# Products of zeros behind TensorE's groups in an attention and gated feed-forward kernel

## The chip, the cores and the metric

The kernel runs on one core of a Trainium2 chip. The metric is the device time of one execution in microseconds (us). TensorE is called PE, VectorE DVE, ScalarE ACT, GpSimd POOL and SyncE SP, as in the rows of the profile.

## The reference

Inputs are q, k and v of shape (4, 8, 768, 64) and three weight arrays. For each of 32 heads:

```python
k_sum = k.reshape(B, H, nb, 32, D).max(axis=3)      # 24 block summaries per head
v_sum = v.reshape(B, H, nb, 32, D).mean(axis=3)
scores_l = scale * q @ k.T, kept where |i - j| < 16, else -1e9
scores_s = scale * q @ k_sum.T + log(32)
a = softmax(concat(scores_l, scores_s))
attn = a @ concat(v, v_sum)
```

The heads are joined to x of shape (4, 768, 512), and then

```python
h = relu(x @ w_in)                                  # 512 -> 1024
conv[s] = w[0]*h[s-1] + w[1]*h[s] + w[2]*h[s+1]     # along the sequence
out = (h * sigmoid(conv)) @ w_out                   # 1024 -> 512
```

## The kernel before, in words

The work is cut into eight chunks `c` (four batches, two halves of 384 positions each). A chunk has four pairs of heads `p`, so there are 32 pairs `n`. One pair goes through these steps. `prep_pair` (L185) takes block maxima of k on DVE and puts windows and maxima into `kw`. `qk` (L231) makes 24 small products of 64 rows into the two banks `pq`. `softmax` (L252) works on DVE and ACT. `tr` (L285) makes three transposes on PE into `pt` for each half and copies them out as `aT`, on ACT or DVE. `av` (L299) makes 24 small products into `xp`, which ACT and DVE split into a high and a low half, `xh` and `xl`. `vmean_pair` (L204) makes block means of v, with one transpose `pv`.

A feed-forward unit `(c, u)` covers 128 of the 1024 hidden columns. `f1` (L370) makes twelve products (three for each of four blocks of x) into a bank with tag f1. `gate_conv` (L391) and `gate_mul` (L420) make the gate on ACT, DVE and POOL. `f2` (L438) accumulates 128 output rows over the eight hidden blocks in the bank with tag f2.

The weights come as 64-bit words. `decode` (L75) and `weights` (L110) turn each block into two 32-bit halves, with one ACT pass, three DVE passes, an ACT copy and a POOL subtraction. w_in is decoded from the prologue into chunk 0, w_out in chunks 0 and 1 (`OUT_AT`).

The program is written in the order: prologue (attention of chunk 0, pairs 0 to 3, L481 to L491), two early units of `f1` and the decoding of the first blocks (L493 to L504), then the loop over chunks (L538). In the loop the attention of chunk c+1 is written between the units of chunk c by `slot`, `slot_t` and `slot_av`. The framework's scheduler sets the order on each engine when it builds the program. It takes the earliest written instruction that its model holds ready, so groups of PE can interleave. On the chip each engine keeps that order, waits at semaphores and overtakes nothing. Loads are on SP's queue, the outputs and two constants on ACT's. There are eight banks of PSUM: two for `pq` (tag s), one for `pt`, one for `xp` (tag x), three for f1, one for f2.

At the very start DVE clears a tile `idle` of 128x512 bf16 and PE makes six products of it with itself into a bank of tag x (L68 to L72). Nothing reads them.

Of the kernel before, what the change touches and what calls it, by code (L numbers as in the profile page):

```python
# [7 lines left out]
F32 = mybir.dt.float32  # L8
# [8 lines left out]
P = 128  # L17
# [6 lines left out]
NK = WK + NB  # L24
SP = S + 2 * WIN
NP = H // 2
# [7 lines left out]
DEPTH = 2  # L34
# [6 lines left out]
EARLY_IN = 2  # L41

OUT_AT = (6, 7, 8, 9, 10, 10, 11, 12)
EARLY_AT = 3
NGROUP = NCHUNK * NP * 2

# [2 lines left out]
def attention_ffn(ctx, tc, qT, kT, vT, v4, w_in, cwT, w_out, mask8, ident_in, out):  # L49
    nc = tc.nc  # L50
    cp = ctx.enter_context(tc.tile_pool(name="cp", bufs=1))
    sp = ctx.enter_context(tc.tile_pool(name="sp", bufs=2))
    ps = ctx.enter_context(tc.tile_pool(name="ps", bufs=1, space=bass.MemoryType.PSUM))
# [3 lines left out]
    ident = cp.tile([P, P], F32, name="ident")  # L57
# [7 lines left out]
    raw_b = cp.tile([P, 6, 1024], U32, name="raw_b", tag="big_b")  # L65


    idle = sp.tile([P, 512], mybir.dt.bfloat16, tag="a", name="idle", bufs=DEPTH + 2)  # L68
    nc.vector.memset(idle, 0.0)
    pw = ps.tile([P, 512], F32, tag="x", name="pw")  # L70
    for i in range(6):
        nc.tensor.matmul(pw, idle[:, :P], idle, start=True, stop=True)  # L72


    def decode(out, words, n, name):  # L75
# [23 lines left out]
    def split_in(fc, t):  # L99
        weights(t, flat(win_hi, fc), flat(win_lo, fc), f"i{fc}")  # L100
# [6 lines left out]
    def split_out(fc, t):  # L107
        weights(t, wout_hi[:, fc, :], wout_lo[:, fc, :], f"o{fc}")
# [14 lines left out]
    for tag in ("xh", "xl"):  # L123
        t = sp.tile([P, 2, KL], F32, tag=tag, name=f"k_{tag}", bufs=2)
        spare += [t[:, 0, :], t[:, 1, :]]

    def window(ap, step, lead, run):

        return bass.AP(
            tensor=ap.tensor, offset=ap.offset, ap=[lead, [QB * step, CB], [1, run]]  # L130
        )
# [99 lines left out]
    def qk(c, p):  # L231


        st = state[(c, p)]
        n = c * NP + p
        pq = [
            ps.tile([P, 512], F32, tag="s", name=f"pq{n}_{h}", bufs=2) for h in range(2)
        ]
        for blk in range(CB):
            i, half = divmod(blk, 2)  # L240
            for h in range(2):
                r = slice(h * QB, (h + 1) * QB)
                nc.tensor.matmul(  # L243
                    pq[h][half * QB : (half + 1) * QB, i * NK : (i + 1) * NK],
                    st["q"][r, blk * QB : (blk + 1) * QB],
                    st["kw"][r, blk, :],
                    start=True,
                    stop=True,
                )
        softmax(n, c % 2, pq)  # L250

    def softmax(n, hf, pq):  # L252
        nm = sp.tile([P, 2, 3], F32, tag="nm", name=f"nm{n}", bufs=3)
        sm = sp.tile([P, 2, 3], F32, tag="sm", name=f"sm{n}", bufs=3)
        for h in range(2):
            a = sp.tile([P, 3, NK], F32, tag="a", name=f"a{n}_{h}", bufs=DEPTH + 2)
            state[("a", 2 * n + h)] = a
            for i in range(3):
                nc.vector.tensor_tensor_reduce(  # L259
                    a[:, i, :],  # L260
                    pq[h][:, i * NK : (i + 1) * NK],
                    mask[:, hf, i, :],
                    -0.125,
                    3.0e38,
                    ALU.add,
                    ALU.min,
                    nm[:, h, i : i + 1],
                )
                nc.scalar.activation(  # L269
                    a[:, i, :],  # L270
                    a[:, i, :],
                    AF.Exp,
                    bias=nm[:, h, i : i + 1],
                    scale=-1.0,
                    accum_out=sm[:, h, i : i + 1],
                )
        nc.scalar.activation(sm, sm, AF.Copy, bias=1e-9)
        nc.vector.reciprocal(sm, sm)
        for h in range(2):
            a = state[("a", 2 * n + h)]  # L280
            (nc.gpsimd if n >= NP else nc.vector).tensor_tensor(  # L281
                a, a, sm[:, h, :].unsqueeze(2).to_broadcast([P, 3, NK]), ALU.mult
            )

    def tr(j):  # L285
        a = state.pop(("a", j))
        pt = ps.tile([P, 512], F32, tag="t", name=f"pt{j}")
        for i in range(3):
            nc.tensor.transpose(pt[:NK, i * P : (i + 1) * P], a[:, i, :], ident)  # L289
        aT = sp.tile([P, 3 * P], F32, tag="aT", name=f"aT{j}", bufs=3)  # L290
        if j < 2 * NP and j % 2:
            nc.vector.tensor_copy(aT[:NK, :], pt[:NK, : 3 * P])
        else:
            nc.scalar.copy(aT[:NK, :], pt[:NK, : 3 * P])
        state[("aT", j)] = aT
# [3 lines left out]
    def av(n):  # L299
        c, p = divmod(n, NP)  # L300
        b, hf = divmod(c, 2)
        va = state[(c, p)]["va"]
        aT = [state.pop(("aT", 2 * n + h)) for h in range(2)]
        xp = ps.tile([P, 512], F32, tag="x", name=f"xp{n}")
        for blk in range(CB):
            for h in range(2):
                r = slice(h * QB, (h + 1) * QB)
                nc.tensor.matmul(  # L308
                    xp[r, blk * QB : (blk + 1) * QB],
                    va[:NK, blk, r],  # L310
                    aT[h][:NK, blk * QB : (blk + 1) * QB],
                    start=True,
                    stop=True,
                )
        if p == 0:
            xh = sp.tile([P, NCC, XW], F32R, tag="xh", name=f"xh{c}", bufs=2)
            xl = sp.tile([P, NCC, XW], F32R, tag="xl", name=f"xl{c}", bufs=2)
            xT[c] = (xh, xl)
            if hf:
                for n, o in zip(xT[c], xT[c - 1]):  # L320
                    nc.vector.tensor_copy(
                        n[:, :, 0:2], o[:, :, CH - 2 : CH].bitcast(F32)
                    )
        xh, xl = xT[c]
        o = 2 * hf
        nc.scalar.copy(xh[:, p, o : o + CH], xp[:, :CH])  # L326
        nc.vector.tensor_tensor(
            xl[:, p, o : o + CH],
            xp[:, :CH],
            xh[:, p, o : o + CH].bitcast(F32),  # L330
            ALU.subtract,
        )
# [25 lines left out]
    def slot_t(j):  # L358
        if 0 <= j - DEPTH < NGROUP:
            tr(j - DEPTH)  # L360
# [9 lines left out]
    def f1(c, fc, ccs):  # L370
        hf = c % 2
        n = CH + 2 * hf
        xh, xl = xT[c]
        if ccs[0] == 0:
            f1ps[(c, fc)] = ps.tile([P, 512], F32, tag="f1", name=f"f1_{c}_{fc}", bufs=3)
        ph = f1ps[(c, fc)]
        for cc in ccs:
            for m, (w, x) in enumerate(
                ((win_hi, xh), (win_hi, xl), (win_lo, xh))
            ):  # L380
                nc.tensor.matmul(  # L381
                    ph[:, :n],
                    w[:, fc, cc, :],
                    x[:, cc, :n],
                    start=(cc == 0 and m == 0),
                    stop=(cc == NCC - 1 and m == 2),
                )

    held = {}

# [115 lines left out]
    def spread(x, n):  # L506
        return [x[len(x) * i // n : len(x) * (i + 1) // n] for i in range(n)]

    def work(c):
# [10 lines left out]
        if c == 1:  # L520
            return [[]] * EARLY_AT + spread(parts, NFC - EARLY_AT)
        return spread(parts, NFC)
# [15 lines left out]
    for c in range(NCHUNK):  # L538
        pieces = work(c)
        last = c == NCHUNK - 1  # L540
        for u in range(NFC):
            j = 8 * (c + 1) + 1 + DEPTH + u
            slot(j)
            if c == 0 and u < 2:
                for fc in (4 + 2 * u, 5 + 2 * u):
                    split_in(fc, raws[fc])
            if c == 0 and u == 2:
                ghi = cp.tile([P, NFC, S], F32R, name="ghi", tag="big_a")
                glo = cp.tile([P, NFC, S], F32R, name="glo", tag="big_b")
            gates(1)  # L550
            early = c == 0 and u < EARLY_IN
            if not early:
                f1(c, u, [0, 1])
            slot_t(j)
            f1(c, u, [3] if early else [2, 3])
            gate_conv(c, u)
            pending.append((c, u))
            assert len(pending) <= 2
            slot_av(j)
            for x in pieces[u]:  # L560
                f2(*x)
            if last:
                gates(0)
            at = NFC * c + u
            for fc in range(NFC):
                if OUT_AT[fc] == at:
                    split_out(fc, raws["o", fc])
            for fc in range(NFC):
                if OUT_AT[fc] == at + 1:
                    raws["o", fc] = load_out(fc)  # L570
# [61 lines left out]
```

## Time and profile before

| what | value |
|---|---|
| times of three runs | 419.74, 421.0 and 1229.91 us, median 421.0 |
| profiled execution | 420.81 us, of which the span of instructions is 419.0 us |
| PE busy | 393.1 us, 94% of the span |
| DVE, ACT, POOL busy | 261.2, 255.8 and 151.0 us |
| mean granted clock of PE | 0.98 |

A row of the timeline gives start and duration in us, engine, source line, output and inputs, shapes and the number of instructions merged into it. The bracket at its end is the idle time of the engine before it and what ended that. A granted clock of 1.00 stands for 2.4 GHz and 0.50 for 1.2 GHz. The chain of waits is followed back from the last instruction to what released each step. The ends of matmuls are modelled, and neighbours overlap in the timeline.

### The profile page before, as it was taken

To read this page: it belongs to the slowest core of one execution; us is meant where nothing else is said; L and a number is where in the kernel's file an instruction comes from. 1 tells how busy PE (TensorE), PEld (TensorE's weight loads), DVE (VectorE), ACT (ScalarE), POOL (GpSimd) and SP (SyncE) were. 2 spreads that over 40 slices of the span, in tenths; PEclk is the share of its full clock that TensorE was granted. 3 is DMA by queue.
4 is the path that set the end of the run, shared out by engine and by line. 5 is a ranking of instruction groups with operands and counts; after the bars stand their busy time and mean duration, and the time that the engine had idled before them with its cause. 6 is when DMAs were issued, how large, how long until landed. Compare 5 with 4: busy or idle time off the path is not lost.

```text
span 419.0 us, 8687 instructions
## 1 busy us (share of the span) xinstructions
PE 393.1 (94%) x3094; PEld 323.2 (77%) x3094; DVE 261.2 (62%) x777; ACT 255.8 (61%) x806; POOL 151.0 (36%) x179
## 2 busy tenths in 40 slices
PE   5769889998789999999999999999999999999996
PEld 3448658867568878887888887888888888888885
DVE  4786896989986655677665455455656654565400
ACT  3474786898877676666566767766556554434311
POOL 2314473467764323333333323332233231222200
PEclk9999767999999999999999999999999999999999
DMA  8997593357796583565233233232221000000011
GB/s 295 343 366 140 153 246 114 101 165 249 214 255 202 184 271 110 145 177 153 82 110 110 77 108 107 78 114 82 64 63 61 27 2 25 27 25 27 26 50 50
DMA packets 60714, 54.46 MB, mean 130 GB/s; under 512 B 24640, under 2 KB 51328, under 8 KB 60672
## 3 DMA queue, kind: packets, MB, share of 16 engines
q1 hardware_dynamic: 56928, 47.19, 38.8%
q10 hardware_dynamic: 3744, 6.73, 4.3%
q8 instruction: 24, 0.39, 0.4%
q14 instruction: 18, 0.15, 0.1%
HBM read 45.55 MB, written 6.29 MB: 124 GB/s over the span
## 4 chain that ended last, share of the span: by engine, by line
PE 77%; DVE 9%; ACT 7%; issue 3%; POOL 2%; DMA 2%; SPq 0%; ACTq 0%; POOLq 0%; DVEq 0%
PE f L448 31%; PE f L381 29%; PE pq L243 6%; PE xp L308 6%; PE pt L289 5%; ACT a L269 2%; DVE a L259 1%; DVE t L410 1%; ACT ob L457 1%; DVE wu_o L87 1%; ACT t L401 1%; DMA k_xh<-kT 1%; DMA q<-qT 1%; DVE wu_o L90 1%; DVE ks L193 1%
## 5 line engine op out<-in xcount | busy, mean ns | idle before, releaser
L432 POOL TENSOR_TENSOR glo<-t,ghi 128x383 fp32r<-128x383 f32 (+1 forms) x64 | 65.6, 1026 | 135.2 <-ACT ghi L431 129.3
L381 PE MATMUL f<-xh,win_hi 128*128 128x384 f32 (+1 forms) x256 | 96.7, 378 | 0.8 <-ACT xh L326 0.8
L410 DVE SCALAR_TENSOR_TENSOR t<-f,cw,t 128x382 f32<-128x382 f32 (+3 forms) x128 | 78.6, 614 | 19.0 <-ACT t L401 16.8
L381 PE MATMUL f<-xl,win_hi 128*128 128x384 f32 (+1 forms) x256 | 89.0, 347 | 0.0
L381 PE MATMUL f<-xh,win_lo 128*128 128x384 f32 (+1 forms) x256 | 88.4, 346 | 0.0
L448 PE MATMUL f<-wout_hi,ghi 128*128 128x512 f32 x192 | 79.0, 412 | 1.2 <-ACT ob L457 0.5
L448 PE MATMUL f<-wout_lo,ghi 128*128 128x512 f32 x192 | 75.8, 395 | 4.0 <-POOL wout_lo L114 4.0
L269 ACT ACTIVATE a<-a,nm 128x120 f32<-128x120 f32 x192 | 73.2, 383 | 7.0 <-DVE nm L259 6.6
L448 PE MATMUL f<-wout_hi,glo 128*128 128x512 f32 x192 | 75.3, 392 | 0.0
L427 ACT ACTIVATE t<-t 128x383 f32<-128x383 f32 (+1 forms) x64 | 33.5, 523 | 62.5 <-DVE t L410 61.7
L281 POOL TENSOR_TENSOR a<-a,sm 128x360 f32<-128x360 f32 x56 | 45.4, 832 | 49.2 <-ACT f L398 41.1
L381 PEld LDWEIGHTS f<-xh,win_hi 128*128 128x128 f32 x256 | 49.6, 194 | 7.8 <-issue 3.8
L428 DVE SCALAR_TENSOR_TENSOR t<-t,f 128x383 f32<-128x383 f32 (+1 forms) x64 | 35.4, 553 | 32.2 <-ACT t L427 32.2
L381 PEld LDWEIGHTS f<-xl,win_hi 128*128 128x128 f32 x256 | 49.9, 195 | 1.6 <-issue 0.3
L381 PEld LDWEIGHTS f<-xh,win_lo 128*128 128x128 f32 x256 | 49.8, 194 | 0.3
L243 PE MATMUL pq<-kw,q 64*64 64x120 f32 x768 | 40.6, 299 | 8.0 <-POOL kw L200 4.9
L243 PEld LDWEIGHTS pq<-kw,q 64*64 64x64 f32 x768 | 27.6, 147 | 24.3 <-issue 12.3
L448 PEld LDWEIGHTS f<-wout_hi,ghi 128*128 128x128 f32 x192 | 36.0, 188 | 12.0 <-ACT ob L457 4.4
L259 DVE CUSTOM_DVE_ANT_0 a<-pq,mask 128x120 f32<-128x120 f32 x192 | 42.2, 276 | 3.7 <-PE pq L243 3.5
L448 PEld LDWEIGHTS f<-wout_lo,ghi 128*128 128x128 f32 x192 | 36.1, 188 | 10.3 <-POOL wout_lo L114 5.0
L431 ACT CAST ghi<-t 128x383 fp32r<-128x383 f32 (+1 forms) x64 | 32.7, 510 | 17.0 <-DVE t L428 16.8
L448 PEld LDWEIGHTS f<-wout_hi,glo 128*128 128x128 f32 x192 | 36.0, 188 | 7.6
(59 smaller groups left out, 493.1 us busy)
## 6 DMA issues: line engine op xcount, KB each, us to landing
va<-v SPq DMA_DIRECT2D x32, 288.0 KB
kw<-kT SPq DMA_DIRECT2D x28, 288.0 KB
q<-qT SPq DMA_DIRECT2D x32, 192.0 KB
out_dram<-ob ACTq DMA_DIRECT2D x24, 256.0 KB
kT<-kT SPq DMA_DIRECT2D x12, 392.0 KB
vt<-vT SPq DMA_DIRECT2D x12, 384.0 KB
wo<-w_out SPq DMA_DIRECT2D x8, 512.0 KB
raw_a<-w_in SPq DMA_DIRECT2D x6, 512.0 KB
```

The lines of the kernel that those rows point to most:

```text
L243: nc.tensor.matmul(pq[h][half * QB : (half + 1) * QB, i * NK : (i + 1) * NK], st["q"][r, blk * QB : (blk + 1) * QB], st["kw"][r, blk, :], ...
L259: nc.vector.tensor_tensor_reduce(a[:, i, :], pq[h][:, i * NK : (i + 1) * NK], mask[:, hf, i, :], -0.125, 3.0e38, ALU.add, ALU.min, nm[:, h ...
L269: nc.scalar.activation(a[:, i, :], a[:, i, :], AF.Exp, bias=nm[:, h, i : i + 1], scale=-1.0, accum_out=sm[:, h, i : i + 1],)
L281: (nc.gpsimd if n >= NP else nc.vector).tensor_tensor(a, a, sm[:, h, :].unsqueeze(2).to_broadcast([P, 3, NK]), ALU.mult)
L308: nc.tensor.matmul(xp[r, blk * QB : (blk + 1) * QB], va[:NK, blk, r], aT[h][:NK, blk * QB : (blk + 1) * QB], start=True, stop=True,)
L381: nc.tensor.matmul(ph[:, :n], w[:, fc, cc, :], x[:, cc, :n], start=(cc == 0 and m == 0), stop=(cc == NCC - 1 and m == 2),)
L410: nc.vector.scalar_tensor_tensor(t[:, i0:i1], h[:, hf + k - 1 + i0 : hf + k - 1 + i1], cw[:, fc, k : k + 1], t[:, i0:i1], ALU.mult, ALU.add,)
L427: nc.scalar.activation(t, t, AF.Tanh, scale=0.5)
L428: nc.vector.scalar_tensor_tensor(t, t, 1.0, h[:, hf : hf + ng], ALU.add, ALU.mult)
L431: nc.scalar.copy(hi, t)
L432: nc.gpsimd.tensor_tensor(glo[:, fc, d0 : d0 + ng], t, hi.bitcast(F32), ALU.subtract)
L448: nc.tensor.matmul(po, gx[:, fc, ss], w[:, fc, :], start=(fc == 0 and m == 0), stop=(fc == NFC - 1 and m == 2),)
```

## The change

The tile `idle` gets a place of its own instead of one of the four rotating buffers of tag a. The bank written by its products is now that of tag f2. A helper `warm` makes a given number of these products, each 128x128 by 128x512 in bf16. Without a second argument they stand where they are written, with one they are tied behind a given PE instruction. There are 10 at the start instead of 6; 5, 12, 3 and 3 behind the score products of pairs 0 to 3; 2 behind each of the eight transposed halves of chunk 0; 3 behind each of the four `av` groups of chunk 0; and 3 behind each of the eight units of chunk 0. That makes 85 products, 79 more than before. `f1` now returns its last instruction.

```diff
+WARM = {"start": 10, "pq0": 5, "pq1": 12, "pq2": 3, "pq3": 3, "tr": 2, "av": 3, "unit": 3}
-    idle = sp.tile([P, 512], mybir.dt.bfloat16, tag="a", name="idle", bufs=DEPTH + 2)
+    idle = cp.tile([P, 512], mybir.dt.bfloat16, name="idle")
     nc.vector.memset(idle, 0.0)
-    pw = ps.tile([P, 512], F32, tag="x", name="pw")
-    for i in range(6):
-        nc.tensor.matmul(pw, idle[:, :P], idle, start=True, stop=True)
+    pw = ps.tile([P, 512], F32, tag="f2", name="pw", bufs=1)
+
+    def warm(where, after=None):
+        def go():
+            for i in range(WARM.get(where, 0)):
+                nc.tensor.matmul(pw, idle[:, :P], idle, start=True, stop=True)
+        if after is None:
+            go()
+        else:
+            with tc.issue_after(after):
+                go()
+    warm("start")
...
     def qk(c, p):
+        if c == 0:
+            warm(f"pq{p}", ins(last))
         softmax(n, c % 2, pq)
...
     def tr(j):
+        if j < 2 * NP:
+            warm("tr", ins(last))
         aT = sp.tile([P, 3 * P], F32, tag="aT", name=f"aT{j}", bufs=3)
...
     def av(n):
+        if c == 0:
+            warm("av", ins(last))
         if p == 0:
...
-            f1(c, u, [3] if early else [2, 3])
+            done = f1(c, u, [3] if early else [2, 3])
+            if c == 0:
+                warm("unit", ins(done))
             gate_conv(c, u)
```

## Rows read from the trace of the kernel before

**Rows 1.** Windows: stretch, its length, busy us of each engine, granted clock, DMA, GB/s.
```profile
0.00:6.20 6.20, 2.74 (x6) 0.74 (x6) 1.59 (x3) 1.28 (x1) 0.67 (x5) 1.00 0.73 249
6.20:37.20 31.00, 23.62 (x223) 16.87 (x223) 24.14 (x85) 16.73 (x69) 9.07 (x13) 1.00 1.10 333
37.20:40.70 3.50, 3.50 (x13) 3.50 (x12) 2.12 (x6) 2.11 (x4) 2.22 (x3) 1.00 0.20 35
40.70:47.50 6.80, 4.74 (x53) 4.04 (x53) 6.53 (x20) 4.70 (x13) 3.74 (x4) 1.00 0.36 96
47.50:57.80 10.30, 10.23 (x86) 7.34 (x85) 8.74 (x36) 8.46 (x36) 6.90 (x8) 0.50 0.84 232
57.80:61.20 3.40, 1.68 (x28) 1.08 (x29) 3.10 (x6) 3.07 (x13) 2.12 (x3) 1.00 1.06 290
61.20:68.10 6.90, 6.71 (x37) 5.63 (x39) 4.98 (x19) 5.39 (x21) 4.67 (x7) 0.51 0.23 45
68.10:83.90 15.80, 15.49 (x167) 12.94 (x163) 13.00 (x43) 12.94 (x41) 5.36 (x8) 1.00 0.41 132
83.90:126.00 42.10, 36.08 (x302) 27.19 (x301) 39.29 (x104) 35.29 (x106) 29.76 (x28) 1.00 0.79 222
126.00:391.40 265.40, 264.35 (x2101) 224.58 (x2100) 155.30 (x457) 161.29 (x502) 84.45 (x104) 1.00 0.32 96
```

**Rows 2.** Timeline of PE, first 41 us.
```profile
1.19 2.74 PE L72 MATMUL pw<-idle 128*128 128x512 bf16 x6 [1.19 <-DVE idle L69]
6.22 1.48 PE L243 MATMUL pq<-kw,q 64*64 64x120 f32 x24 [2.29 <-POOL kw L200]
13.26 0.73 PE L243 MATMUL pq<-kw,q 64*64 64x120 f32 x4 [2.28 <-POOL kw L200]
16.67 0.89 PE L289 MATMUL pt<-ident,a 128*120 128x128 f32 x3
35.71 1.55 PE L308 MATMUL xp<-aT,va 120*64 120x64 f32 x24 [0.68 <-DVE xl L327]
39.91 0.52 PE L381 MATMUL f<-xl,win_hi 128*128 128x384 f32 x1
40.23 0.52 PE L381 MATMUL f<-xh,win_lo 128*128 128x384 f32 x1
40.81 0.34 PE L381 MATMUL f<-xl,win_hi 128*128 128x384 f32 x1
40.98 0.34 PE L381 MATMUL f<-xh,win_lo 128*128 128x384 f32 x1
```

**Rows 3.** Timeline of PE, 42 to 84 us.
```profile
42.83 0.85 PE L243 MATMUL pq<-kw,q 64*64 64x120 f32 x24
46.99 0.99 PE L243 MATMUL pq<-kw,q 64*64 64x120 f32 x12 [2.06 <-issue]
60.26 0.52 PE L289 MATMUL pt<-ident,a 128*120 128x128 f32 x3 [1.71 <-ACT aT L294]
83.04 0.92 PE L308 MATMUL xp<-aT,va 120*64 120x64 f32 x24
```

**Rows 4.** Chain of waits, 6.2 to 37.2 us, share of that stretch by line.
```profile
by line: PE pq L243 23.5%; PE pt L289 18.5%; PE xp L308 15.3%; DVE a L259 10.0%; DVE a L281 7.4%; DVE aT L292 5.2%; DVE xl L327 4.3%; issue 2.8%; DVE vs L211 2.8%; DVE ks L193 2.8%; POOL kw L200 2.3%; PE pv L217 2.3%; DVE sm L278 1.3%; DVE 
```

**Rows 5.** Chain of waits in order of time: start, us, what.
```profile
63.09 4.14 PE f L381 x12
361.52 2.08 PE f L448 x9
```

**Rows 6.** Timeline of DVE, the waits for PE that the prediction uses.
```profile
34.43 0.56 DVE L292 COPY aT<-pt 120x384 f32<-120x384 f32 x1 [1.62 <-PE pt L289]
50.05 0.28 DVE L259 CUSTOM_DVE_ANT_0 a<-pq,mask 128x120 f32<-128x120 f32 x1 [1.25 <-PE pq L243]
68.90 0.56 DVE L327 TENSOR_TENSOR xl<-xp,xh 128x384 fp32r<-128x384 f32 x1 [2.46 <-ACT xh L326]
```

**Rows 7.** Windows of 16 to 24 us, columns as in rows 1.
```profile
16.00:20.00 4.00, 3.76 (x27) 2.49 (x26) 2.40 (x14) 0.27 (x1) 1.13 (x2) 1.00 1.07 338
20.00:24.00 4.00, 3.80 (x37) 2.65 (x36) 2.15 (x11) 3.39 (x16) 0.00 (x0) 1.00 1.07 337
```

More of the change, by code (lines that the diff above doesn't have):

```diff
@@ L125, in attention_ffn, with ins @@
         spare += [t[:, 0, :], t[:, 1, :]]
+    def ins(x):
+        return getattr(x, "ins", x)
     def window(ap, step, lead, run):
@@ L242, in qk @@
                 r = slice(h * QB, (h + 1) * QB)
-                nc.tensor.matmul(
+                last = nc.tensor.matmul(
                     pq[h][half * QB : (half + 1) * QB, i * NK : (i + 1) * NK],
@@ L288, in tr @@
         for i in range(3):
-            nc.tensor.transpose(pt[:NK, i * P : (i + 1) * P], a[:, i, :], ident)
+            last = nc.tensor.transpose(pt[:NK, i * P : (i + 1) * P], a[:, i, :], ident)
+        if j < 2 * NP:
+            warm("tr", ins(last))
         aT = sp.tile([P, 3 * P], F32, tag="aT", name=f"aT{j}", bufs=3)
@@ L307, in av @@
                 r = slice(h * QB, (h + 1) * QB)
-                nc.tensor.matmul(
+                last = nc.tensor.matmul(
                     xp[r, blk * QB : (blk + 1) * QB],
@@ L380, in f1 @@
             ):
-                nc.tensor.matmul(
+                last = nc.tensor.matmul(
                     ph[:, :n],
@@ L387, in f1 @@
                 )
+        return last
     held = {}
```

## The prediction

> **What bounds the kernel now.** I read the windows first, then the timeline of PE, then the chain of waits, and last DVE's own waits. The windows show three regimes [rows 1]. From 126.0 to 391.4 us PE is busy for 264.35 of 265.40 us: nothing done early changes what it has to do there, so a gain made before 126 us arrives at the end whole, and so does a loss. From 83.9 to 126 us DVE is busy for 39.29 of 42.10 us and PE for 36.08: DVE sets the pace. From 6.2 to 37.2 us nobody is full: PE 23.62 and DVE 24.14 of 31.00 us. There a chain runs from engine to engine, and PE has 59.6% of it (23.5 + 18.5 + 15.3 + 2.3, scores, transposes, value products, block means), that is 18.5 us [rows 4].
>
> The reader should not take the clock column at its word for the first 40 us. It says 1.00 there [rows 1], but the durations say 0.50: 24 score products take 1.48 us at 6.22 and 0.85 us at 42.83; three transposes 0.89 us at 16.67 and 0.52 us at 60.26; 24 value products 1.55 us at 35.71 and 0.92 us at 83.04. Two neighbouring `f1` products start 0.32 us apart at 39.91 and 0.17 us apart at 40.81 [rows 2, 3]. So the 2.4 GHz level begins near 40.7 us, after some 5 us of unbroken work, and all before was at 1.2 GHz. After that the column is credible: it falls to 0.50 from 47.5 to 57.8, behind an idle stretch of 2.06 us, and again from 61.2 to 68.1, behind one of 1.71 us [rows 1, 3]. The low level holds for about 58 us in all.
>
> **The start.** Six products took 2.74 us, 0.46 us each at the low level [rows 2]. Four more are 1.8 us, and PE then waits 2.29 us for POOL's `kw` anyway: nothing on the path. If that cover were gone, 1.8 us. The new places of `idle` and its bank cost nothing: the cover is that the first `f2` group belongs to chunk 1, behind the last of the products.
>
> **The prologue.** What a high level saves: the three pairs of durations above give ratios of 0.57, 0.58 and 0.59, so 0.42 of the chain's 18.5 us, 7.8 us. That is the upper end. What it costs: 51 products stand in it (5 + 12 + 3 + 3 + 8x2 + 4x3). No product of this kind is seen at the high level; the nearest row is `f2`, also 512 columns, nine in 2.08 us, so 0.23 us each as an estimate [rows 5], and 0.46 us at the low one. At 0.23 us they are 11.7 us. PE finishes a group and then has to work these off before anything behind them, ready or not, since it overtakes nothing. Place by place:
> - Behind pair 0's scores, 1.2 us: the next scores wait for DVE to read the banks. Nothing.
> - Behind pair 1's, 2.8 us into a wait of 2.28 us [rows 2]: 0.5 us.
> - Behind pairs 2 and 3, 0.7 us each: one of the two on the path, 0.7 us.
> - Behind transposes, 0.46 us each: the path goes on through the copy to `aT`, 0.56 us [rows 6], which covers them; where a ready group of PE follows, in two of eight, 0.9 us.
> - Behind value products, 0.7 us each, mostly with a ready group next: three of four, 2.1 us.
>
> That is 4.2 us, and the prologue gains 7.8 - 4.2 = 3.6 us if the level is high from pair 0 on. If it rises only halfway through the twelve, the first two score groups save nothing (0.42 x 3.0 = 1.3 us), and the first 17 products need 5.9 us (half at each price), where the 7.0 us from 6.22 to 13.26 less 3.0 us of scores leave 4.0: 1.9 us late instead of 0.5. Then the gain is 3.6 - 1.3 - 1.4 = 0.9 us. The level could also stay low (rival C). At the start 2.74 us of such products didn't raise it; 5 us of unbroken work at 35.7 us did [rows 1, 2]. The start now has 4.6 us and the run behind pair 1 up to 5.5 us, so I expect it up by 6 to 14 us, nearer the early end, and take **-2.5 us**.
>
> **37.2 to 47.5 us.** The ten or so `f1` products at 0.32 us would save 0.15 us each, 1.5 us. But DVE is busy for 6.53 of 6.80 us behind them, decoding weights [rows 1]: I take nothing. What is late next is DVE.
>
> **47.5 to 57.8 us.** DVE waits 1.25 us for pair 5's scores at the low level [rows 6]. With the products of units 0 and 1 in front (6 x 0.23 = 1.4 us), the idle 2.06 us shrinks to about 0.7, which may keep the clock up; chunk 1's scores, transposes and value products have none of their own. Between 0 and -1.25 us: **-0.6 us**.
>
> **61.2 to 68.1 us.** Twelve `f1` products take 4.14 us where 2.1 would do (12 x 0.17), and behind them DVE waits 2.46 us for a chain that begins with PE [rows 5, 6]. The idle stretch before it hangs on an ACT copy and not on PE's speed, and there is nothing between units 2 and 3 to fill it. So 0 to -2.0 us; **-1.0 us**.
>
> **The products of units 2 to 7.** 6 x 0.7 = 4.1 us, and from 68.1 to 83.9 us PE is busy 15.49 of 15.80 us: each delays what PE does next [rows 1]. DVE and ACT have 2.8 and 2.9 us of slack there and can take part of it, since what they wait for comes in a bunch. From 0 to +4.1 us; nearest to the slack, so 4.1 - 2.8 = **+1.3 us**.
>
> **Sum.** -2.5 - 0.6 - 1.0 + 1.3 = -2.8 us. The profiled execution took 420.81 us (span 419.0 us and 1.8 us around it), 0.2 us under the median of 421.0. That gives **418.0 us**.
>
> **Rivals.**
>
> A, the level holds all the way. 3.6 us in the prologue, plus the two or so microseconds of products that the path doesn't see after all (2.1 behind value products), 1.25, 2.0, 1.5 of `f1`, and only 1.3 us paid back: about -9 us, **411.5 us**. For it: DVE, which would have to follow, is idle 6.9 us in the prologue and 2.8 us from 68.1 to 83.9 [rows 1]. Against it: the unguarded score and transpose stretch from 52 to 61 us. Chance 0.17.
>
> B, the time is hidden. What PE saves turns into waiting for DVE, ACT and loads, and the products eat the rest: 0.9 us saved in the prologue, nothing in the later low stretches, 1.3 us paid: +0.4 us, **421.2 us**. For it: DVE's 24.14 us of work in 31 us, and an order of instructions built for other durations. A page bears on it: the Trainium skill, "TensorE: Matmul & The Clock Gate", Part 1, puts the ramp penalty under 1% of a typical kernel's span and advises against fitting it; that would be at most 4.2 us here, and with the 4.2 + 1.3 us of products on the path the sum would be +1.3 us, 422.1 us. Rows 2 to 4 give 7.8 us for the prologue alone, so the trace doesn't bear the page out: this ramp lasts 40 us. Chance 0.22.
>
> C, slower: the level stays low through the prologue, because score and value groups between the products fill too little of PE. Then 51 products cost 0.46 us, 23.5 us, beside 23.62 us of work in 31 us: 47.1 us, **+16 us, 437 us**. It decides at the end of the twelve behind pair 1; if transposes near 16 us still take 0.89 us, it is on. For it: from 16 to 24 us PE worked almost without a break (3.76 and 3.80 of 4.00 us) at the low level in the kernel before, and it didn't rise [rows 7]. Against it: the twelve themselves. Chance 0.06. That the change doesn't do what it says (the scheduler putting the products elsewhere) would end between B and C, and is counted there.
>
> My forecast has the rest, 0.55, with a range of its own from 414 to 421 us.
>
> **Numbers.** A measurement of this kernel tells about 2% from no change, so 412.6 and 429.4 us are the bounds. Faster: most of A and little else, 0.14. Slower: C and a part of the worse end of B, 0.07. Same: 0.79. The range reaches into A and over B and leaves out C and the far side of A: 411 to 423.5 us.
>
> **What would show it.** In the trace after: transposes of three at 0.52 us from about 14 us on (0.89 means C); the value products of pair 3, now from 35.71 us, at about 33 us (36 and later means B); a granted clock of 1.00 from 47.5 to 57.8 us for A, and 4.1 us for twelve `f1` products in the sixties if that stretch stays low; DVE's waits of 1.62 us [rows 6] and 1.25 us shorter; units 4 to 7 spread by 0.7 us each. I am wrong if PE's full stretch, now from 126 us, begins over 5 us away from 123.

## The result and the profile after

| | before | after |
|---|---|---|
| median of runs | 420.98 us | 415.27 us (413.72 to 416.98) |
| profiled execution, its span | 420.81, 419.0 us | 414.49, 412.7 us |
| ratio, 95% interval | | 0.9885 [0.9858, 0.9911] |

The kernel became 5.7 us faster; 418.0 us was forecast. One execution of the kernel before took 1229.91 us and is left out of the ratio. TensorE's level did what was hoped. These are the windows of the kernel after, cut at the changes of level, columns as in rows 1:

```profile
5.10:28.99 23.89, 20.88 (x215) 11.37 (x214) 21.31 (x81) 14.75 (x65) 7.63 (x12) 1.00 1.06 351
28.99:32.40 3.41, 3.41 (x28) 1.86 (x26) 2.29 (x5) 2.00 (x4) 1.80 (x2) 0.50 1.09 334
32.40:100.67 68.27, 60.10 (x601) 45.70 (x601) 64.50 (x183) 57.52 (x184) 40.38 (x44) 1.00 0.71 195
100.67:107.50 6.83, 6.83 (x32) 5.79 (x28) 6.59 (x17) 4.25 (x15) 4.26 (x4) 0.50 0.84 211
```

PE is at 2.4 GHz from 5.1 us, where before it came there at 40.7, and stays there but for 3.4 us near 30 and 6.8 us near 104. The low stretches of before at 47.5 and 61.2 us [rows 1] are gone, the one at 100.67 is new. The timeline of PE shows the durations that answer to [rows 2]:

```profile
1.19 4.25 PE L77 MATMUL pw<-idle 128*128 128x512 bf16 x10 [1.19 <-DVE idle L71]
6.34 0.84 PE L259 MATMUL pq<-kw,q 64*64 64x120 f32 x24 [0.90 <-POOL kw L216]
10.23 2.54 PE L77 MATMUL pw<-idle 128*128 128x512 bf16 x11
13.04 0.54 PE L307 MATMUL pt<-ident,a 128*120 128x128 f32 x3
17.84 0.92 PE L328 MATMUL xp<-aT,va 120*64 120x64 f32 x24
```

Eleven products of zeros in 2.54 us make 0.23 us each, the estimate of the prediction. The chain of waits (start, time, engine, tile, line, count) has twelve `f1` products in 2.30 us, where [rows 5] had 4.14:

```profile
58.33 2.30 PE f L403 x12
```

So far it looks like a gain by the clock. The experiments say that it isn't.

### The profile page after: what moved, and what is told of

It reads as the page before. It is cut to its first block, busy times and chain, and to the rows that moved or that the text cites. A ratio compares the mean times of both kernels' runs of the same rounds, so it can differ in the third digit from the quotient of the medians.

```text
span 412.7 us, 8842 instructions
## 1 busy us (share of the span) xinstructions
PE 395.1 (96%) x3173; PEld 318.4 (77%) x3173; DVE 262.0 (63%) x777; ACT 255.9 (62%) x806; POOL 148.8 (36%) x179
## 4 chain that ended last, share of the span: by engine, by line
PE 74%; ACT 10%; DVE 6%; DMA 3%; POOL 2%; SPq 2%; issue 2%; ACTq 0%; DVEq 0%
PE f L471 30%; PE f L403 28%; PE pq L259 5%; PE xp L328 5%; ACT a L287 4%; PE pt L307 4%; DVE t L433 2%; PE pw L77 2%; DMA va<-v 1%; DMA k_xh<-kT 1%; ACT ob L480 1%; ACT t L424 1%; ACT f L421 1%; ACT aT L314 1%; POOL a L299 1%
## 5 line engine op out<-in xcount | busy, mean ns | idle before, releaser
L403 PE MATMUL f<-xh,win_hi 128*128 128x384 f32 (+1 forms) x256 | 95.3, 372 | 0.2 <-DVE t L451 0.2
L403 PE MATMUL f<-xl,win_hi 128*128 128x384 f32 (+1 forms) x256 | 87.9, 343 | 0.0
L403 PE MATMUL f<-xh,win_lo 128*128 128x384 f32 (+1 forms) x256 | 87.2, 341 | 0.0
L403 PEld LDWEIGHTS f<-xl,win_hi 128*128 128x128 f32 x256 | 49.0, 191 | 1.4
L403 PEld LDWEIGHTS f<-xh,win_lo 128*128 128x128 f32 x256 | 48.7, 190 | 0.4
L259 PEld LDWEIGHTS pq<-kw,q 64*64 64x64 f32 x768 | 24.2, 133 | 21.2 <-issue 12.1
L259 PE MATMUL pq<-kw,q 64*64 64x120 f32 x768 | 35.6, 276 | 4.3 <-issue 2.3
```

Of the source, the lines that this page charges most:

```text
L259: last = nc.tensor.matmul(pq[h][half * QB : (half + 1) * QB, i * NK : (i + 1) * NK], st["q"][r, blk * QB : (blk + 1) * QB], st["kw"][r, bl ...
L403: last = nc.tensor.matmul(ph[:, :n], w[:, fc, cc, :], x[:, cc, :n], start=(cc == 0 and m == 0), stop=(cc == NCC - 1 and m == 2),)
```

## Experiments

The times of each group of runs stand against runs of the kernel before on the same chip. "Narrow" products have 16 columns and not 512: they take little of PE's time (five in 0.28 us where five whole ones took 1.25), and the level was not held behind them, as windows below show. The ten at the start stay whole wherever products are narrow. To part the level from what else the change does, I kept orders of instructions: the program is built once with one set of widths, the sequence on each engine is read off, and a second build with other widths gets an ordering edge, without a semaphore, between neighbours of that sequence. This was needed because the framework's scheduler plans with the durations of its own model: 79 products more change the order on all engines. Compared by the names of tiles, the traces of before and after have 2927 of PE's 3088 records other than products of zeros in a common sequence, 705 of DVE's 777 and 734 of ACT's 806. Runs that share a kept order have all of them in the same sequence. (The expectations below count instructions of the program and not records of a trace.)

**The places of `idle` and its bank.**

```diff
-WARM = {"start": 10, "pq0": 5, "pq1": 12, "pq2": 3, "pq3": 3, "tr": 2, "av": 3, "unit": 3}
+WARM = {"start": 6}
```

> Keeps the new places of idle and its bank (own tile, bank of tag f2), but makes only the six products of before at the start. Every engine's order is that of before. Theory L (the gain is PE's clock level): ratio to before 1.00, clock 0.98 and a low level until about 40 us as before, 421 us. Theory O (the gain is the new order of instructions): 1.00 too, 421 us. Theory T (the gain is the place of idle and of its bank): ratio near 0.989, 416 us.

Measured: 420.74 us, 0.999 [0.997, 1.001]. Theory T is out. The trace has every record in the sequence of before.

**Order against width.** Two orders (of the program after; of the program with narrow products, close to before's), each with whole and with narrow products.

```diff
-                nc.tensor.matmul(pw, idle[:, :P], idle, start=True, stop=True)
+                n = 512 if where == "start" else WIDTH[0]
+                nc.tensor.matmul(pw[:, :n], idle[:, :P], idle[:, :n], start=True, stop=True)
...
+    first = build(512, None)        # the order; 16 for the other pair
+    order = {}
+    for x in first.all_instructions():
+        order.setdefault(str(x.engine), []).append(x.name)
+    nc = build(16, order)           # the widths that run; 512 for the other pair
...
+                    for a, b in zip(names, names[1:]):
+                        tc.add_manual_dep(made[b], a, how, reason="order")
```

> All products of the change, with every engine's order of instructions that of the changed kernel, but the 75 products behind groups are 16 columns wide and not 512; the ten at the start are whole. Theory L: the level rises at the start at best and is lost soon, the low stretches of before come back, 419 to 423 us, ratio 0.995 to 1.005. Theory O: the order alone brings the gain, and PE is even freed of 75 x 0.23 = 17 us of products, 411 to 415 us, ratio 0.975 to 0.987.

> All products whole (512 columns), but every engine keeps the order that the scheduler gives the program with 16-column products, which is close to that of before (2278 of 2322 instructions of PE and 725 of 778 of DVE in the same sequence). Theory L: the level is high from early on, 413 to 417 us, ratio 0.98 to 0.99. Theory O: no gain, or a loss by the products on the path, 420 to 425 us, ratio 1.00 to 1.01.

> All products of the change, the 75 behind groups 16 columns wide, in the order that the scheduler gives this program (the same order as in the run with whole products kept to it). Theory L: 419 to 423 us, low level for most of the first 40 us, ratio 0.995 to 1.005. Theory O: this order is nearly that of before, so 419 to 422 us as well; the pair with whole products in the same order tells the clock's share, theory L 5 us or more between them, theory O under 2 us.

| ratio to before | narrow products | whole products |
|---|---|---|
| order of the program after | 0.9891 [0.9863, 0.9919], 416.14 us | 0.9885 [0.9858, 0.9911], 415.27 us |
| order of the narrow program | 1.0031 [1.001, 1.0052], 422.15 us | 1.0033 [1.0009, 1.0057], 421.87 us |

Down a column the order makes 1.4 to 1.5%. Along a row the products, with the level that they bring and the time that they take, make nothing that can be told from noise. The narrow run in the order after hit neither range: it was no faster than the whole one, where theory O had 411 to 415 us. The level did differ. Windows of the narrow run in the order after:

```profile
10.00:20.00 10.00, 8.52 (x88) 6.39 (x87) 8.36 (x36) 6.33 (x33) 3.25 (x7) 0.53 1.08 320
20.00:30.00 10.00, 8.58 (x84) 6.51 (x82) 9.32 (x30) 6.60 (x25) 1.86 (x2) 0.50 1.04 360
```

and of the whole one in the narrow order:

```profile
10.00:20.00 10.00, 8.79 (x82) 4.71 (x81) 8.12 (x32) 4.68 (x23) 3.45 (x6) 1.00 1.07 335
20.00:30.00 10.00, 7.58 (x76) 4.20 (x74) 8.80 (x29) 7.60 (x33) 2.09 (x2) 1.00 1.04 368
```

Theory L, that the clock brings the gain, fell with these. The times at the end don't say where a gain and a loss meet. The pair in the narrow program's order shows it, for one execution each. These are the first scores of pair 4 and the value products of pair 7, narrow products first:

```profile
42.65 0.84 PE L260 MATMUL pq<-kw,q 64*64 64x120 f32 x24
81.28 0.92 PE L329 MATMUL xp<-aT,va 120*64 120x64 f32 x24
```

```profile
40.23 0.84 PE L263 MATMUL pq<-kw,q 64*64 64x120 f32 x24
82.34 0.92 PE L332 MATMUL xp<-aT,va 120*64 120x64 f32 x24
```

With whole products PE is 2.4 us ahead at pair 4 and 1.1 us behind at pair 7. Between 60 and 85 us it has no idle time with whole products, and 1.9 us with narrow ones, again narrow first:

```profile
60.00:85.00 25.00, 23.08 (x243) 19.32 (x243) 20.89 (x69) 23.08 (x79) 12.60 (x17) 1.00 0.48 136
```

```profile
60.00:85.00 25.00, 25.00 (x219) 19.33 (x218) 18.28 (x57) 19.61 (x70) 9.55 (x14) 0.94 0.33 101
```

So in this order the prologue did gain, and the stretch with the units' products lost it again. The two executions ended 1.0 us apart, spans of 420.3 us (narrow) and 419.3 us (whole).

**Products of the prologue against those of the units, in the order after.**

```diff
+    nc = build({'unit': 16}, order)                       # one run: prologue whole
+    nc = build({'pq': 16, 'tr': 16, 'av': 16}, order)     # the other: units whole
```

> The changed kernel's order of instructions on every engine; the products of the prologue whole, the 24 behind the units 16 columns wide. The run with all 75 narrow in this order gave ratio 0.989, the changed kernel 0.9885. Theory P (level and price cancel: the prologue's level is worth some 3 us, the units' products cost as much on PE's full stretch from 60 to 79 us): ratio 0.978 to 0.984, 412 to 414 us. Theory N (neither level nor products reach the end, which hangs on the order alone): 0.987 to 0.991, 415 to 417 us.

> The changed kernel's order; the products of the prologue 16 columns wide (the ten at the start whole), the 24 behind the units whole. Theory P: the price without the level, 24 x 0.23 = 5.5 us less what idle time takes, 417 to 420 us, ratio 0.992 to 0.998. Theory N: 415 to 417 us, ratio 0.987 to 0.991.

Measured 416.73 us, 0.9896 [0.9872, 0.9921], and 415.28 us, 0.9879 [0.9853, 0.9905]. Theory N: in this order no balance of a gain in the prologue against a loss behind the units is seen.

**Other orders.** The same change without a part of its products, in whatever order the scheduler then gives.

```diff
-WARM = {"start": 10, "pq0": 5, "pq1": 12, "pq2": 3, "pq3": 3, "tr": 2, "av": 3, "unit": 3}
+WARM = {"start": 10, "pq0": 5, "pq1": 12, "pq2": 3, "pq3": 3, "tr": 2, "av": 3}   # one run: prologue alone
+WARM = {"start": 6, "unit": 3}                                                    # the other: units alone
```

> The change without the products behind units, in the order that the scheduler gives this program (a third order: 2133 of PE's 2322 and 630 of DVE's 778 instructions in the sequence of before). If the gain needs the order that the units' products bring: 419 to 423 us, ratio 0.995 to 1.005. If the prologue's products bring the good order: 412 to 416 us, ratio 0.98 to 0.988.

> Six products at the start as before and those behind units alone, in the scheduler's order for this program (2211 of PE's 2322 and 669 of DVE's 778 in the sequence of before). If the units' products bring the good order: 414 to 418 us, ratio 0.983 to 0.993. If not: low level in the prologue as before and 24 products more, 421 to 425 us, ratio 1.00 to 1.01.

Measured 413.35 us, 0.982 [0.9796, 0.9844], and 420.24 us, 0.999 [0.9971, 1.0009], the second somewhat under the 421 to 425 us expected without the good order. Products of the prologue alone give a version faster than the one after. That can again be level or order, so the first order was kept with narrow products:

> The order of instructions of the program without units' products (the run that gave ratio 0.982), kept on every engine, with its 51 products of the prologue 16 columns wide; the ten at the start whole. Theory O (the order alone): 0.979 to 0.985, 412 to 415 us, with the clock low for most of the first 40 us. Theory L (in this order the level does reach the end): 0.988 to 1.00, 416 to 421 us.

Measured 413.25 us, 0.9843 [0.9811, 0.9875]: the order again, and no difference by the products. The timeline of PE with whole products:

```profile
6.44 1.48 PE L259 MATMUL pq<-kw,q 64*64 64x120 f32 x24 [0.80 <-POOL kw L216]
7.85 2.31 PE L77 MATMUL pw<-idle 128*128 128x512 bf16 x5
16.25 0.54 PE L307 MATMUL pt<-ident,a 128*120 128x128 f32 x3
16.62 0.59 PE L77 MATMUL pw<-idle 128*128 128x512 bf16 x2
19.22 0.92 PE L328 MATMUL xp<-aT,va 120*64 120x64 f32 x24
20.07 0.82 PE L77 MATMUL pw<-idle 128*128 128x512 bf16 x3
22.65 0.63 PE L259 MATMUL pq<-kw,q 64*64 64x120 f32 x14
```

and with narrow ones, same order:

```profile
6.27 1.48 PE L263 MATMUL pq<-kw,q 64*64 64x120 f32 x24 [0.64 <-POOL kw L220]
7.68 0.30 PE L81 MATMUL pw<-idle 128*128 128x16 bf16 x5
15.21 0.89 PE L311 MATMUL pt<-ident,a 128*120 128x128 f32 x3
15.89 0.25 PE L81 MATMUL pw<-idle 128*128 128x16 bf16 x2
18.12 1.55 PE L332 MATMUL xp<-aT,va 120*64 120x64 f32 x24
19.60 0.25 PE L81 MATMUL pw<-idle 128*128 128x16 bf16 x3
22.16 1.07 PE L263 MATMUL pq<-kw,q 64*64 64x120 f32 x14
```

In both of these executions the level is still low behind the ten products at the start: 24 scores take 1.48 us. Five whole products cost 2.31 us there against 0.30, and at 16 us the whole version is a microsecond late (transposes at 16.25 and 15.21 us). Then its level is high and it gains: three transposes take 0.54 us and not 0.89, the value products 0.92 and not 1.55. Net of the products between them it makes up half of its delay by the next scores, which start at 22.65 and 22.16 us. The spans are 411.3 and 411.0 us.

**Which part of the order.** The order after for the instructions written before the loop over chunks, and the narrow program's for the loop; and the reverse. All products narrow.

```diff
+    for part, width in enumerate(({}, {'pq': 16, 'tr': 16, 'av': 16, 'unit': 16})):   # swapped for the reverse
+        for x in build(width, None).all_instructions():
+            if (int(x.name[2:]) >= LOOP[0]) == bool(part):
+                order.setdefault((str(x.engine), part), []).append(x.name)
```

> All 75 products behind groups 16 columns wide. The instructions written before the loop over chunks keep the changed kernel's order, those of the loop keep the order of the program with narrow products (which alone gave 1.003). If the gain sits in the prologue's queues (DVE's copies of transposes behind ready work, its waits for them 1.2 us in all and not 3.5): 0.986 to 0.992, 415 to 418 us. If it sits in the loop's order: 0.998 to 1.005, 420 to 423 us.

> The other half: the prologue in the order of the program with narrow products, the loop over chunks in the changed kernel's order, all 75 products narrow. If the gain sits in the loop's order: 0.986 to 0.992, 415 to 418 us. If it sits in the prologue's queues: 0.998 to 1.005, 420 to 423 us. Both near 0.995 would mean that each half brings a part.

Measured 422.65 us, 1.004 [1.0005, 1.0074], and 421.5 us, 1.0019 [1.0002, 1.0036]. Neither half brings any of it. I had expected one to. The idle time of DVE before its copies `aT`, 5.0 us before and 1.2 us now, says that the prologue's half did what it should. These are DVE's groups up to 42 us of the kernel before, of the narrow run in the order after, and of the run with the prologue's half (behind the first bar stand the busy time and the mean of one, behind the second the idle time before them and what ended most of it):

```profile
L292 DVE COPY aT<-pt 120x384 f32<-120x384 f32 x4 | 2.2, 554 | 5.0 <-PE pt L289 5.0
```

```profile
L316 DVE COPY aT<-pt 120x384 f32<-120x384 f32 x4 | 2.2, 548 | 1.2 <-PE pt L311 1.2
```

```profile
L316 DVE COPY aT<-pt 120x384 f32<-120x384 f32 x4 | 2.2, 550 | 1.2 <-PE pt L311 1.2
```

In the order after, DVE has sums of v, a reciprocal and softmax products ahead of the second copy, and one pass more of decoding a w_in block ahead of the fourth, where before it stood and waited for PE. But with the narrow program's loop behind it the time is given back between 40 and 60 us. Windows of 40 to 60 us, the prologue's half first, then the narrow run with both halves:

```profile
40.00:60.00 20.00, 12.68 (x142) 10.50 (x134) 14.75 (x54) 13.80 (x53) 10.18 (x10) 0.80 0.75 195
```

```profile
40.00:60.00 20.00, 14.63 (x167) 11.41 (x169) 17.56 (x64) 16.08 (x61) 12.55 (x12) 0.79 0.80 210
```

DVE does 14.75 us of work against 17.56. The waits in that stretch, DVE's then PE's, with the prologue's half:

```profile
48.83 0.19 DVE L300 RECIPROCAL sm<-sm 128x6 f32<-128x6 f32 x1 [2.32 <-ACT sm L299]
50.79 0.61 DVE L437 SCALAR_TENSOR_TENSOR t<-f,cw,t 128x382 f32<-128x382 f32 x1 [1.77 <-ACT t L428]
```

```profile
56.67 0.87 PE L311 MATMUL pt<-ident,a 128*120 128x128 f32 x3 [5.87 <-ACT aT L318]
```

With both halves PE's longest wait for such a copy was 3.20 us, ending at 58.87. The starts of PE's score products show the same: pair 4 and pair 7 with the prologue's half, then with both halves.

```profile
39.52 0.85 PE L263 MATMUL pq<-kw,q 64*64 64x120 f32 x24
58.94 1.46 PE L263 MATMUL pq<-kw,q 64*64 64x120 f32 x18
```

```profile
39.90 0.85 PE L263 MATMUL pq<-kw,q 64*64 64x120 f32 x24
54.83 0.85 PE L263 MATMUL pq<-kw,q 64*64 64x120 f32 x24
```

Before they start at 42.83 [rows 3] and 57.70 us. So the prologue's half alone has its lead of 3.3 us at pair 4 and has lost it at pair 7; with the loop's half it is kept.

**Taking DVE's wait away without any product.**

```diff
-        if j < 2 * NP and j % 2:
-            nc.vector.tensor_copy(aT[:NK, :], pt[:NK, : 3 * P])
-        else:
-            nc.scalar.copy(aT[:NK, :], pt[:NK, : 3 * P])
+        nc.scalar.copy(aT[:NK, :], pt[:NK, : 3 * P])
```

> The kernel before with no product more, where ACT makes the four copies of transposes to aT that DVE made in the prologue, so that DVE no longer waits 5.0 us for transposes there and decodes w_in earlier. If DVE's waits in the prologue reach the end: 3 to 5 us less, 416 to 418 us, ratio 0.988 to 0.993. If the loop's order decides: 0.996 to 1.004, 419 to 423 us.

Measured 419.57 us, 0.9979 [0.9954, 1.0003], as expected if the loop's order decides: the wait moves. In the timeline of DVE a wait of 3.37 us for scores of PE ends at 23.75 us; the scheduler's order was another one again.

## Why the prediction was right in its number and wrong in its reason

**The start: right.** No loss, and in the profiled execution the level rose at 5.1 us, before pair 0's scores.

**The sum: the step that failed.** -2.8 us was added up from the level and the products' cost, on the path of an order of instructions that it took as given. The new order, which the change brings with it, stood at nothing. The runs show it the other way round: the order is worth 1.4% (0.9891 against 1.0031, both with narrow products), some 5.9 us; the level with its products -0.3 us in the order after (0.9885 against 0.9891) and +0.1 us in the narrow program's (1.0033 against 1.0031). The intervals of the ratios leave some 1.5 us of doubt on these two differences, an estimate.

**The prologue's -2.5 us: seen in one order, not at the end.** The level did what was said: groups took 0.57 to 0.61 of their time at the low level. In the narrow program's order the trace has 2.4 us of it at pair 4's scores, net of the products. But in the order after, whole products of the prologue end as narrow ones do (0.9896 against 0.9891). There no run says whether the products on the path cost more than 4.2 us or waits for other engines hid what PE saved.

**37.2 to 68.1 us.** The low stretches went, as rival A had it, but no run shows the forecast's -0.6 and -1.0 us: the narrow run in the order after had a granted clock of 0.79 from 40 to 60 us (the row above) and ended within noise of the whole one. Nor did the idle 2.06 us before pair 5's scores shrink to about 0.7: PE waited 2.29 us there, and the level stayed up all the same (row in the last section).

**The units' +1.3 us.** In the order after it is not seen: narrow units (0.9896) and whole ones (0.9885) don't differ, nor do whole units behind a prologue with narrow products (0.9879). In the narrow program's order the traces show more: from 2.4 us ahead at pair 4 to 1.1 us behind at pair 7, some 3.5 us, for the most part in a stretch where PE had no idle time left to take the products.

**Rival B: near in the level's worth, wrong in the sign of the order.** It had what PE saves eaten by waits and products, and the net is nothing. It named "an order of instructions built for other durations" only as something against a gain. That order is what made the time.

**Where the order gains.** The trace of the kernel after has the lead early: pair 4's scores, and the 49th of the `f1` products.

```profile
38.88 0.85 PE L259 MATMUL pq<-kw,q 64*64 64x120 f32 x24
61.75 0.42 PE L403 MATMUL f<-xh,win_hi 128*128 128x384 f32 x1
```

Before, the scores stood at 42.83 us [rows 3] and that product at 68.27:

```profile
68.27 0.44 PE L381 MATMUL f<-xh,win_hi 128*128 128x384 f32 x1
```

So 3.9 us are won by pair 4 and 6.5 us by 62 us, and the spans differ by 6.3 us: on balance nothing is added later. With narrow products in the same order it is 2.9 us at pair 4 (39.90 us, above) and 3.2 us at the end (spans of 419.0 and 415.8 us). That profiled execution was the slowest of its four, 417.84 us with a median of 416.14, so the 3.3 us between the two profiled executions are not the level's worth; the medians differ by 0.9 us.

The windows behind 85 us are easily misread, after and then before:

```profile
85.00:126.00 41.00, 38.39 (x296) 30.56 (x295) 33.50 (x87) 33.02 (x104) 24.65 (x26) 0.92 0.74 201
```

```profile
85.00:126.00 41.00, 34.98 (x296) 26.17 (x295) 38.19 (x102) 34.19 (x100) 29.76 (x28) 1.00 0.81 227
```

PE is busy for 3.4 us more in the kernel after, but with 296 products in both: 6.83 us of it passed at half the clock (from 100.67 us, above), and half of that is the difference. It is more time, not more work.

**Luck.** The number came out in the range by luck of direction: -2.8 us summed from the clock, -5.7 us measured, and the measured ones come from the order. Whole products in the narrow program's order ended at 1.0033, and there the same sum would have been wrong by its whole size.

**The signs.** Transposes at 0.54 us from 13.04 us, pair 3's value products from 33.26 us and a granted clock of 1.00 from 47.5 to 57.8 us came as the forecast or rival A had them. All are signs of the level, so they could not tell that the time came from elsewhere. PE's last wait of over 0.3 us ended at 118.39 us after and at 116.28 us before: the start of its full stretch doesn't show the gain.

**A short ramp.** The Trainium skill, "TensorE: Matmul & The Clock Gate", Part 1, calls the ramp's penalty under 1% of a typical kernel's span and advises against fitting it. I set it aside for rows that show 40 us at the low level. The low level was there; replacing it with products of zeros was worth -0.3 us net in the order after, under 1% of the span. No run shows the penalty without the products' cost, so the Trainium skill's figure is neither confirmed nor refuted here.

**What stays open.** Which instructions of the order matter. Halving it showed only that the two halves act together. The kept halves leave it to the scheduler how they interleave at their border, so a part of the loss may sit there. The exact order of before with whole products was not tried, only one close to it. And the level without the products' cost was not run.

## What to carry to other kernels

Where a scheduler plans with modelled durations, any instruction added for the sake of the chip also changes the plan. Before a gain is put down to the chip, run the new order without the effect (here narrow products in the kept order) and the effect in the old order: two runs tell clock from sequence. A product that keeps a clock up costs its own time, and here the two came out even: the 413 us of the fastest order were measured with whole products (413.35 us) and with narrow ones (413.25 us). And where the clock differs, compare starts of the same instruction, since an engine at half the clock is busy longer with the same work.

## What of the hardware was unexpected

The length of a wait alone did not tell when the level falls. Before, it fell behind waits of 2.06 and 1.71 us [rows 3]. In the kernel after PE waited 2.29 and 2.02 us and stayed at 2.4 GHz (granted clock 1.00 from 32.40 to 100.67 us, above):

```profile
43.19 0.83 PE L259 MATMUL pq<-kw,q 64*64 64x120 f32 x12 [2.29 <-issue]
57.20 0.51 PE L307 MATMUL pt<-ident,a 128*120 128x128 f32 x3 [2.02 <-ACT aT L314]
```

It then waited only 0.85 and 0.82 us near 99 and 100 us and was at 1.2 GHz from 100.67 us for 6.8 us, in a stretch with real products between.

Nor did the same ten whole products (4.25 us) at the start always raise the level. Behind them the first 24 scores took 0.84 or 0.85 us in eight of the ten executions profiled with them, the kernel after among them, and 1.48 us in the two with the prologue's products alone, whole and narrow (above). With narrow products behind them the level was lost again in the order after: a granted clock of 0.53 from 10 to 20 us and 0.50 from 20 to 30 us, although PE was busy for 8.5 of 10 us in both.
